# Silus of a Strassen-like first product queued behind the next copies, and one add ahead of the accumulators' sums

## The chip, the cores and the metric

The kernel runs on one core of a Trainium2 chip. The metric is the device time of one execution in microseconds (us). The numbers of the trace come from one profiled execution; its rows name TensorE as PE (its weight loads as PEld), VectorE as DVE, ScalarE as ACT, GpSimd as POOL, and the queue that issues DMAs as SP.

## The reference

Two blocks follow each other. The first is a chunked state-space scan over 4 batches of 8 heads with 768 positions; its output, laid out as 3072 tokens by 256 features, goes through a product to 2048 hidden features, the quick form of gelu, and a product back to 256.

```python
# per batch and head, chunk by chunk (32 positions), state is 16 x 32
L = np.exp(cum[:, :, :, None] - cum[:, :, None, :]) * causal
M = np.einsum('bhin,bhjn->bhij', Cc, Bc) * L
y = M @ xc + (Cc @ state) * exp(cum)
state = decay_full * state + sum_j(Bc_j xc_j * decay_from_j)
...
x = attn_out.transpose(0, 2, 1, 3).reshape(3072, 256)
h = x @ w_in                                  # 256 -> 2048
g = h * (1.0 / (1.0 + np.exp(-1.702 * h)))    # silu(1.702 h) / 1.702
out = (g @ w_out).astype(np.float32)          # 2048 -> 256
```

All is fp32.

## The kernel before

The 3072 tokens are worked off in six groups of 512 (g = 0 to 5). For each group the scan block makes yT (the tokens' features, transposed), the first product makes gT (the hidden features behind the silu), and the second product adds gT times w_out up in accumulators in PSUM. Within each engine the instructions run in the order in which the code is written; nothing reorders them. So the order is a matter of the strings of steps in the code.

Groups 2 to 5 do both products with seven instead of eight multiplications of half blocks (Winograd's form of Strassen's). The 2048 hidden features are eight pairs of blocks, j = 0 to 7. For one pair the first product has seven TensorE steps, written j.1, j.6, j.7, j.4 (into the PSUM tile X, one after the other; the partial sum after 1, 6 and 7 is copied by ScalarE to ac[0], b and ac[1], so that step 6 can't write X until the copy after step 1 has read it) and j.5, j.2, j.3 (into the PSUM tile Y). Step j.4 ends with a silu from X. Step j.D is no product: VectorE adds Y and ac into two quarters of gT, and ScalarE puts the silu over them. After j.3, which adds into Y once more and so must follow that add, VectorE adds Y and b into another quarter, and ScalarE puts the silu over it. Each TensorE step shows as two rows of 128x256 in the trace, since fp32 matmuls count double.

The second product of a pair is seven accumulations, each a P in the strings; they need gT and its differences, which VectorE makes in `mix_g` (tile mg, an M in the strings). Because P lags some pairs behind, the accumulations of the last two pairs of group g-1 stand among the first steps of group g. When they are all in, `combine` (C) adds the seven accumulators up: `copies` copies two of them on ScalarE (tile u), then VectorE does five adds (tiles u and c). `give` transposes c and stores it.

The PSUM holds one area of four banks that serves in turn as accumulators of a group (acc) and for the scan block's products cb (`score`; s1 and s2 in the strings); VectorE's `weigh` (w1, w2) multiplies cb into L. The other four banks rotate among X, Y and the rest (tag ff). y1 to y3 are the scan block's products that give yT of the next group. `decay` (2.3 us on VectorE) is called once per pass of the loop over the later pairs in groups 2 and 3. `clip_rows` and `decay_rows` make, once in group 2, the running product of a batch row of `a`, which `turn` needs for group 4 (tile since, read into CsT). The loads of later groups and the stores are issued by SP in the order of the code.

The start of a group, as it is before:

```python
run(g, "0.1 P P 0.6 P P 0.7 P 0.5 P 0.2 P 0.D", seven(g - 1, 6))
run(g, "1.1 P 0.4 P P 1.6 P P 0.3 M P P C 1.7 1.5 1.2 1.D", seven(g - 1, 7),
    M=lambda: mix_g(g, 0), C=lambda: combine(g - 1))
```

## Time and profile before

| what | value |
|---|---|
| median of 3 runs | 412.14 us (407.86 to 413.92) |
| the profiled execution | 409.75 us |
| its span, first to last instruction | 408.0 us |
| TensorE busy | 380.8 us, 93% of the span |
| VectorE busy | 272.5 us, 67% |
| ScalarE busy | 148.6 us, 36% |
| mean granted TensorE clock | 0.983 |

The profiled execution lies 2.4 us under the median. Rows of the timeline give the start from the span's beginning, the duration, engine, line, operation, tiles (out<-in), shape, how many instructions were merged, and in brackets the idle time before with the engine that ended it. In the clock line of the page a digit is the granted clock in tenths of full speed, in 40 slices of 10.2 us; 9 stands for full speed too.

### The profile page before, as it was taken

How to read it: one execution, taken by the hardware profiler on the slowest of the kernel's cores; microseconds unless marked ns; L12 is line 12 of the kernel's file. 1: busy time of each engine (PE TensorE's matmuls, PEld its weight loads, DVE VectorE, ACT ScalarE, POOL GpSimd, SP SyncE). 2: the span in 40 equal slices, each digit the busy share in tenths (PEclk: the TensorE clock that was granted, in tenths of full speed). 3: DMA queues.
4: the chain of work that ended last, by engine and by line, in shares of the span. 5: the costliest groups of instructions: out<-in, count | busy, mean ns of one | idle time of the engine just before them, and what ended most of it. 6: DMA issues, size and time to landing. Idle time of an engine off the chain costs nothing.

```text
span 408.0 us, 5632 instructions
## 1 busy us (share of the span) xinstructions
PE 380.8 (93%) x2216; PEld 282.3 (69%) x2216; DVE 272.5 (67%) x440; ACT 148.6 (36%) x330; POOL 10.4 (3%) x32
## 2 busy tenths in 40 slices
PE   6989999999999997899999699999699999689995
PEld 2444358885566786577878477888567888568885
DVE  3999999997799795446795456785454354433453
ACT  3338643303322222534333253433343432343430
POOL 5000000100000100000000000000000000000000
PEclk9999999999999999899999899999989999989999
DMA  8988947707683000085100062000010000000011
GB/s 140 234 233 196 287 154 85 222 12 132 139 169 116 16 24 0 26 185 101 51 2 2 0 119 90 0 0 2 0 53 0 2 1 0 2 0 0 2 51 51
DMA packets 85793, 29.55 MB, mean 72 GB/s; under 512 B 75720, under 2 KB 79240, under 8 KB 85768
## 3 DMA queue, kind: packets, MB, share of 16 engines
q1 hardware_dynamic: 85672, 29.07, 30.2%
q8 instruction: 17, 0.28, 0.3%
q10 hardware_dynamic: 96, 0.13, 0.1%
q14 instruction: 8, 0.07, 0.1%
HBM read 25.95 MB, written 3.24 MB: 72 GB/s over the span
## 4 chain that ended last, share of the span: by engine, by line
PE 80%; DVE 13%; issue 3%; ACT 2%; DMA 1%; POOL 0%; ACTq 0%; POOLq 0%; DVEq 0%
PE acc L742 27%; PE X L649 13%; PE h L593 13%; PE Y L659 10%; PE o L685 7%; PE cb L472 3%; DVE L L483 3%; PE y L549 2%; DVE gT L759 2%; PE y L540 1%; PE tp L436 1%; PE ab L331 1%; DVE c L759 1%; DVE u L759 1%; DVE mg L618 1%
## 5 line engine op out<-in xcount | busy, mean ns | idle before, releaser
L627 ACT ACTIVATE gT<-gT 128x512 f32<-128x512 f32 x64 | 33.5, 524 | 97.9 <-DVE gT L759 97.9
L742 PE MATMUL acc<-mg,mw 128*128 128x256 f32 x240 | 65.3, 379 | 0.0
L593 PE MATMUL h<-yT,w_in 128*128 128x512 f32 x128 | 57.4, 596 | 0.8 <-DVE w_in L186 0.8
L649 PE MATMUL X<-my,mi 128*128 128x256 f32 x128 | 41.9, 410 | 15.6 <-ACT ac L654 15.4
L759 DVE TENSOR_TENSOR gT<-Y,ac 128x512 f32<-128x512 f32 x32 | 22.0, 689 | 46.2 <-PE Y L659 45.4
L742 PEld LDWEIGHTS acc<-mg,mw 128*128 128x128 f32 x240 | 45.4, 190 | 6.1
L759 DVE TENSOR_TENSOR gT<-Y,b 128x256 f32<-128x256 f32 x32 | 13.5, 422 | 52.3 <-PE Y L659 52.3
L593 PEld LDWEIGHTS h<-yT,w_in 128*128 128x128 f32 x128 | 23.7, 190 | 29.3 <-issue 25.0
L742 PE MATMUL acc<-gT,w_out 128*128 128x256 f32 x160 | 43.8, 380 | 0.0
L323 DVE TENSOR_TENSOR_SCAN L<-a,idents 128x1024 f32<-128x1024 f32 x18 | 41.1, 2284 | 0.0
L649 PEld LDWEIGHTS X<-my,mi 128*128 128x128 f32 x128 | 23.1, 195 | 24.3 <-ACT ac L654 19.1
L654 ACT ACTIVATE ac<-X 128x256 f32<-128x256 f32 x64 | 24.1, 376 | 28.1 <-PE X L649 28.1
L596 ACT ACTIVATE gT<-h 128x512 f32<-128x512 f32 x32 | 19.0, 594 | 41.0 <-PE h L593 40.7
L742 PEld LDWEIGHTS acc<-gT,w_out 128*128 128x128 f32 x160 | 29.9, 190 | 5.3 <-issue 1.4
L483 DVE TENSOR_TENSOR L<-L,cb 128x2048 f32<-128x2048 f32 (+1 forms) x13 | 27.5, 2122 | 4.8 <-PE cb L472 4.3
L685 PE MATMUL o<-w_out,gT 128*128 128x256 f32 x128 | 29.3, 383 | 0.0
L618 DVE TENSOR_TENSOR mg<-gT 128x512 f32<-128x512 f32 x40 | 27.3, 683 | 1.9 <-ACT gT L627 1.9
L685 PEld LDWEIGHTS o<-w_out,gT 128*128 128x128 f32 x128 | 23.8, 190 | 4.1 <-issue 0.7
L742 PE MATMUL acc<-gT,mw 128*128 128x256 f32 x80 | 23.7, 382 | 0.0
L742 PE MATMUL acc<-mg,w_out 128*128 128x256 f32 x80 | 23.5, 379 | 0.0
L649 PE MATMUL X<-yT,w_in 128*128 128x256 f32 x64 | 19.7, 390 | 1.6 <-ACT yT L571 0.9
L659 PE MATMUL Y<-yT,mi 128*128 128x256 f32 x64 | 20.9, 411 | 0.0
(112 smaller groups left out, 518.7 us busy)
## 6 DMA issues: line engine op xcount, KB each, us to landing
a<-scratch SPq DMA_DIRECT2D x18, 512.0 KB, 5.8
bits<-in_moe_w_out_dram SPq DMA_DIRECT2D x4, 1024.0 KB, 7.1
x<-in_x_dram SPq DMA_DIRECT2D x24, 128.0 KB, 3.2
out_dram<-ob SPq DMA_DIRECT2D x11, 256.0 KB, 2.2
bits<-in_moe_w_in_dram SPq DMA_DIRECT2D x4, 512.0 KB
bits<-in_moe_w_in_dram SPq DMA_DIRECT2D x2, 1024.0 KB
b<-in_B_dram SPq DMA_DIRECT2D x24, 64.0 KB, 4.9
c<-in_C_dram SPq DMA_DIRECT2D x24, 64.0 KB, 2.8
```

The costliest lines, as they stand in the source:

```text
L323: nc.vector.tensor_tensor_scan(out=Ls[p][:, k].rearrange("p r q i -> p (r q i)"), data0=ra[n], data1=idents.rearrange("p h i -> p (h i)"), ...
L483: nc.vector.tensor_tensor(out=Lv[:, k], in0=Lv[:, k], in1=cb.rearrange("p r k e -> p k r e")[:, k], op=ALU.mult)
L593: nc.tensor.matmul(out=h, lhsT=w_in[:, k, f * P:(f + 1) * P], rhs=yT[g][:, k], start=(k == 0), stop=(k == NK - 1))
L596: nc.scalar.activation(gT[g, j][:, i], h, AF.Silu, scale=GELU_SCALE)
L618: nc.vector.tensor_tensor(out=t[:, 0:2], in0=B[:, :, 1], in1=B[:, 0], op=ALU.subtract)
L627: nc.scalar.activation(o, i, AF.Silu, scale=GELU_SCALE)
L649: nc.tensor.matmul(out=s["X"], lhsT=lhsT, rhs=rhs, start=i == "1", stop=i == "4", skip_group_check=True)
L654: nc.scalar.activation(copy, s["X"], AF.Copy)
L659: nc.tensor.matmul(out=o, lhsT=lhsT, rhs=rhs, start=s.pop("new", False), stop=i != "5", skip_group_check=True)
L685: nc.tensor.matmul(out=o[k // 2][:, k % 2], lhsT=gT[g, f // 2][:, f % 2, k * P:(k + 1) * P], rhs=w_out[:, f], start=(f == 0 and k % 2 == 0 ...
L742: nc.tensor.matmul(out=acc[g][0][i], lhsT=lhsT, rhs=rhs, start=(j == 0 and i in (0, 2, 5, 6)), stop=(j == NF // 2 - 1), skip_group_check=True)
L759: nc.vector.tensor_tensor(out=o, in0=v, in1=w, op=ALU.add)
```

## The change

The silu of j.D becomes a step of its own, j.S, and the silu after j.3 a step j.T. Both then stand later in the strings: S behind the next pair's step 1, T behind the next pair's step 7 (or a step near it). At a group's start 1.D is written ahead of C, 1.3 moves up behind 1.4, 0.3 moves up by one P, and 2.7 and 2.2 change places, as do 1.7 and a P. `clip_rows` and `decay_rows` move from behind pair 7 of group 2 to ahead of pair 4. Nothing is added or removed: each engine has as many instructions as before.

```diff
             if i == "3":
-                c12 = gT[g, j][:, 0, HT:]
-                plus(c12, s["Y"][:, 1], s["b"])
-                silu(c12, c12)
+                plus(gT[g, j][:, 0, HT:], s["Y"][:, 1], s["b"])
+        elif i == "T":
+            c12 = gT[g, j][:, 0, HT:]
+            silu(c12, c12)
         else:
-            block(g, j)
+            if i == "D":
+                block(g, j)
             c = gT[g, j].rearrange("p i (t e) -> p (i t) e", t=2)[:, 0:4:3]
-            plus(c, s["Y"], s["ac"])
-            silu(c, c)
+            if i == "D":
+                plus(c, s["Y"], s["ac"])
+            else:
+                silu(c, c)
...
-        run(g, "1.1 P 0.4 P P 1.6 P P 0.3 M P P C 1.7 1.5 1.2 1.D", seven(g - 1, 7),
+        run(g, "1.1 0.S P 0.4 P P 1.6 P 0.3 0.T M P P 1.7 P 1.5 1.2 1.D C", seven(g - 1, 7),
             M=lambda: mix_g(g, 0), C=lambda: combine(g - 1))
...
-            run(g, "2.1 1.4 2.6 2.5 2.7 2.2 1.3 s1 2.D w1 2.4 give 2.3 3.1 s2 w2 3.6 y1 3.7 y2 y3 3.5 "
-                "3.2 3.D", s1=lambda: score(n), w1=lambda: weigh(n), give=lambda: give(g - 1),
+            run(g, "2.1 1.S 1.4 1.3 2.6 2.5 2.2 2.7 1.T s1 2.D 2.S w1 2.4 give 2.3 3.1 2.T s2 w2 3.6 "
+                "y1 3.7 y2 y3 3.5 3.2 3.D", s1=lambda: score(n), w1=lambda: weigh(n), give=lambda: give(g - 1),
...
-            run(g, "P P 3.4 P P 3.3 P P P M", seven(g, 0), M=lambda: mix_g(g, 1))
+            run(g, "P P 3.S 3.4 P P 3.3 3.T P P P M", seven(g, 0), M=lambda: mix_g(g, 1))
+            for r in rows:
+                clip_rows(r)
+                decay_rows(r)
...
-            run(g, "2.1 1.4 2.6 2.5 2.7 2.2 1.3 2.D 3.1 2.4 3.5 3.6 2.3 3.2 3.7 3.D M",
+            run(g, "2.1 1.S 1.4 1.3 2.6 2.5 2.2 2.7 1.T 2.D 3.1 2.S 2.4 3.5 3.6 2.3 3.2 3.7 2.T 3.D M",
...
-            h = "{1}.1 P {0}.4 P {1}.6 P {0}.3 P {1}.7 P {1}.5 P {1}.2 P {1}.D M".format(j - 1, j)
+            h = "{1}.1 {0}.S P {0}.4 P {1}.6 P {0}.3 P {1}.7 {0}.T P {1}.5 P {1}.2 P {1}.D M".format(j - 1, j)
...
-        run(g, f"P P {k}.4 P P {k}.3 P P P", seven(g, 4))
+        run(g, f"P {k}.S P {k}.4 P P {k}.3 {k}.T P P P", seven(g, 4))
...
         mix_g(g, 6)
-        for b in rows:
-            clip_rows(b)
-            decay_rows(b)
```

What this does to ScalarE's queue at the start of group 3 (gT_0 and gT_1 are the group's first two pairs, ac and b the copies of X, u the copies of the accumulators), before:

```order
L627 ACTIVATE gT_0_1651<-gT_0_1651 128x256
L752 ACTIVATE u_1677<-acc_1373 128x2x256
L654 ACTIVATE ac_1_1655<-X_1_1654 128x256
L627 ACTIVATE gT_1_1690<-gT_1_1690 128x2x256
L654 ACTIVATE ac_2_1694<-X_2_1693 128x256
L627 ACTIVATE gT_1_1690<-X_1_1654 128x256
```

and with the change:

```order
L627 ACTIVATE gT_0_1651<-gT_0_1651 128x256
L655 ACTIVATE ac_1_1654<-X_1_1653 128x256
L757 ACTIVATE u_1684<-acc_1372 128x2x256
L655 ACTIVATE ac_2_1693<-X_2_1692 128x256
L627 ACTIVATE gT_1_1682<-gT_1_1682 128x2x256
L627 ACTIVATE gT_1_1682<-X_1_1653 128x256
```

The copy of 2.1 (ac_2) has changed places with silu 1.S (gT_1 over itself), and the copy of 1.7 (ac_1) with that of the accumulators.

VectorE's queue at the same place, from the last of mg_0 on, before:

```order
L620 TENSOR_TENSOR mg_0_1671<-gT_0_1651,mg_0_1671 128x256
L759 TENSOR_TENSOR u_1677<-acc_1373,u_1677 128x256
L759 TENSOR_TENSOR u_1677<-acc_1373,u_1677 128x512
L759 TENSOR_TENSOR c_1678<-u_1677 128x256
L759 TENSOR_TENSOR c_1678<-acc_1373,u_1677 128x512
L759 TENSOR_TENSOR c_1678<-acc_1373,u_1677 128x256
L759 TENSOR_TENSOR gT_1_1690<-Y_1_1687,ac_1_1655 128x2x256
```

and with the change:

```order
L620 TENSOR_TENSOR mg_0_1670<-gT_0_1651,mg_0_1670 128x256
L764 TENSOR_TENSOR gT_1_1682<-Y_1_1679,ac_1_1654 128x2x256
L764 TENSOR_TENSOR u_1684<-acc_1372,u_1684 128x256
L764 TENSOR_TENSOR u_1684<-acc_1372,u_1684 128x512
L764 TENSOR_TENSOR c_1685<-u_1684 128x256
L764 TENSOR_TENSOR c_1685<-acc_1372,u_1684 128x512
L764 TENSOR_TENSOR c_1685<-acc_1372,u_1684 128x256
```

The add of 1.D (gT_1) has moved from behind the five sums to ahead of them.

TensorE at the same place, from 1.4 to cb, before:

```order
L649 MATMUL X_1_1654<-my_1573,w_in 128x256
L649 MATMUL X_2_1693<-my_1573,mi_769 128x256
L659 MATMUL Y_2_1702<-my_1573,mi_769 128x256
L649 MATMUL X_2_1693<-my_1573,mi_769 128x256
L659 MATMUL Y_2_1702<-yT_1331,w_in 128x256
L659 MATMUL Y_1_1687<-yT_1331,mi_764 128x256
L472 MATMUL cb_1710<-CT_1568,BT_1566 128x256 x8
```

and with the change:

```order
L650 MATMUL X_1_1653<-my_1573,w_in 128x256
L660 MATMUL Y_1_1679<-yT_1331,mi_764 128x256
L650 MATMUL X_2_1692<-my_1573,mi_769 128x256
L660 MATMUL Y_2_1704<-my_1573,mi_769 128x256
L660 MATMUL Y_2_1704<-yT_1331,w_in 128x256
L650 MATMUL X_2_1692<-my_1573,mi_769 128x256
L472 MATMUL cb_1710<-CT_1568,BT_1566 128x256 x8
```

Step 1.3 (into Y_1) now stands directly behind 1.4, ahead of 2.6, and the last two steps into X_2 and Y_2 have changed places.

## The prediction

> **What bounds the kernel now.** I read the page first, then TensorE's waits, then the timeline of one start of a token group, then windows of the clock.

> ```profile
> span 408.0 us, 5632 instructions
> PE 380.8 (93%) x2216; PEld 282.3 (69%) x2216; DVE 272.5 (67%) x440; ACT 148.6 (36%) x330; POOL 10.4 (3%) x32
> PEclk9999999999999999899999899999989999989999
> PE 80%; DVE 13%; issue 3%; ACT 2%; DMA 1%; POOL 0%; ACTq 0%; POOLq 0%; DVEq 0%
> PE X L649 <- ACT ac L654: 15.4, 6, 3.6
> ```

> TensorE is busy for 93% of the span and holds 80% of the chain, so the time falls only where TensorE waits or runs slowly. The last row is from its waits (total, times, longest): of all its waiting behind other engines 15.4 us stand in six waits of an X product for a copy by ScalarE. The clock line has four 8s, in slices 17, 23, 30 and 36, one to each of groups 2 to 5. The timeline shows one of the long waits, at the start of group 3 (start, duration, engine and line, in brackets the idle time before):

> ```profile
> 222.45 0.59 PE L659 MATMUL Y<-yT,mi 128*128 128x256 f32 x2
> 223.08 0.42 DVE L759 TENSOR_TENSOR gT<-Y,b 128x256 f32<-128x256 f32 x1 [3.56 <-PE Y L659]
> 223.54 0.42 ACT L627 ACTIVATE gT<-gT 128x256 f32<-128x256 f32 x1 [1.37 <-DVE gT L759]
> 223.99 0.69 DVE L618 TENSOR_TENSOR mg<-gT 128x512 f32<-128x512 f32 x1 [0.48 <-ACT gT L627]
> 224.61 0.59 PE L659 MATMUL Y<-yT,w_in 128*128 128x256 f32 x2
> 225.04 0.59 PE L649 MATMUL X<-yT,w_in 128*128 128x256 f32 x2
> 225.47 0.59 PE L649 MATMUL X<-my,w_in 128*128 128x256 f32 x2
> 225.52 1.14 DVE L759 TENSOR_TENSOR u<-acc,u 128x256 f32<-128x256 f32 x2
> 227.97 0.68 DVE L759 TENSOR_TENSOR gT<-Y,ac 128x512 f32<-128x512 f32 x1
> 228.69 0.63 ACT L627 ACTIVATE gT<-gT 128x512 f32<-128x512 f32 x1 [3.87 <-DVE gT L759]
> 229.22 0.37 ACT L654 ACTIVATE ac<-X 128x256 f32<-128x256 f32 x1
> 229.64 0.70 PE L649 MATMUL X<-my,mi 128*128 128x256 f32 x2 [3.57 <-ACT ac L654]
> 233.67 1.22 PE L472 MATMUL cb<-CT,BT 32*128 32x256 f32 x16
> 234.97 2.29 DVE L483 TENSOR_TENSOR L<-L,cb 128x2048 f32<-128x2048 f32 x1 [0.17 <-PE cb L472]
> ```

> From the bottom up: product 2.6 (229.64) waits for the copy of 2.1 (229.22). That copy's input was ready long before: in these rows an engine that reads a product starts 0.63 us after the product does (222.45 to 223.08), so 225.04 + 0.63 = 225.67. But in ScalarE's queue silu 1.S stands ahead of it, and 1.S waits for add 1.D (227.97), which stands on VectorE behind the five sums of the accumulators (from 225.52). Step to step TensorE takes 0.43 us (225.04 to 225.47), so 2.6 was due at 225.90: it is 3.74 us late. Afterwards TensorE runs at half rate:

> ```profile
> 226.00:229.60 3.60, 0.07 (x1) 0.00 (x0) 2.62 (x5) 0.92 (x3) 0.00 (x0) 1.00 0.00 0
> 230.50:233.90 3.40, 3.40 (x12) 2.08 (x14) 0.12 (x1) 0.64 (x2) 0.00 (x0) 0.50 0.00 0
> ```

> Here the first pair of numbers behind the window is its length and TensorE's busy time; the third from the right is the granted clock. An empty stretch of 3.6 us is followed by 3.4 us at 0.50, which does 1.7 us less work.

> **The change at the start of a group.** I lay the new order over the same rows, with group 3's times.
> - TensorE, one step each 0.43 us: 0.3 comes one step earlier, at 222.02; 1.7 at 223.31; the last accumulation of the group before at 223.75; 1.5, 1.2, 2.1, 1.4 keep 224.18, 224.61, 225.04, 225.47; 1.3 is due at 225.90.
> - VectorE: the add of 0.3 begins at 222.02 + 0.63 = 222.65, silu 0.T 0.46 later (223.08 to 223.54) at 223.11, the three differences mg_0 0.45 after that, at 223.56; they take 225.52 - 223.99 = 1.53, to 225.09. Add 1.D follows a Y step by 0.71, so 224.61 + 0.71 = 225.32, for 0.61 to 0.69. The sums start at 225.93 and take 227.97 - 225.52 = 2.45: their last ends at about 228.45. So they are 0.4 us later than now.
> - ScalarE: copy 2.1 at 225.67, with no silu ahead of it that is still waiting. Product 2.6 follows a copy's start by 0.42 (229.22 to 229.64): 226.09 at the earliest. In its queue stands 1.3, which adds into the Y that 1.D reads, so it starts at 226.05 instead of 225.90, and 2.6 at 226.5, 2.5, 2.2, 2.7 at 226.9, 227.3, 227.8. Silus 1.S (0.72 after 1.D: 226.05) and 1.4 end before 2.6's copy is ready at 227.1, so 2.7 isn't held.
> - The next thing that is late is the cb products, due at 228.2: their PSUM area is that of the accumulators, and the sums must have read it. They start at about **228.5**, a new wait of 0.3.

> From there on nothing changes in relation to cb: the weighing (234.97, 1.30 after cb) has 1.3's and 2.D's adds ahead of it, which fit into 228.4 to 229.6; output copies, stores and the loads queued on SP behind the stores come as much sooner as the rest. So a group start gains 233.67 - 228.5 = **5.2 us**: 3.74 of the wait, and 1.88 between 2.6 and cb, where five steps now take 4.03 us instead of 2.15, less 0.45 for the two new short waits (0.15 at 1.3, 0.3 at cb). Groups 2, 3 and 4 have the same pattern: **15.5**. What I don't see is the price of cb behind the sums: none if the sums keep up, and up to 1.5 more if mg_0's 1.53 came between; I take 0.3, from 2.45 us of sums in these rows. For three groups that is -0.9 to +3.6 us.

> **The last group** has no cb products, and two more short waits:

> ```profile
> 356.15 0.70 PE L649 MATMUL X<-my,mi 128*128 128x256 f32 x2 [3.57 <-ACT ac L654]
> 362.30 0.70 PE L649 MATMUL X<-my,mi 128*128 128x256 f32 x2 [0.74 <-ACT ac L654]
> 364.00:366.00 2.00, 2.00 (x10) 1.44 (x8) 1.25 (x2) 1.24 (x3) 0.00 (x0) 1.00 0.00 0
> 366.43 0.70 PE L649 MATMUL X<-my,mi 128*128 128x256 f32 x2 [0.41 <-ACT ac L654]
> ```

> (The third row is a window's.) The times are group 3's plus 126.5 (356.15 against 229.64), so its 2.6 comes at 353.0. From there to 4.6 stand 15 steps (2.5, 2.2, 2.7, 3.1, 2.4, 3.5, 3.6, 2.3, 3.2, 3.7, 4.1, three between, 4.6) at 0.43, 6.45 us; one step, 2.4, waits 0.2 for the copy of 2.7. That makes 359.65 against 366.43: **6.8 us**, of which 5.5 are the pattern above without the wait at cb, and 1.15 the two short waits.

> **The scan of a's row** runs once, in group 2 (VectorE's rows; the X product is 0.1 of group 3):

> ```profile
> 181.56 0.42 DVE L620 TENSOR_TENSOR mg<-gT,mg 128x256 f32<-128x256 f32 x1
> 185.18 0.69 DVE L759 TENSOR_TENSOR gT<-Y,ac 128x512 f32<-128x512 f32 x1 [3.20 <-PE Y L659]
> 210.51 0.55 DVE L378 TENSOR_SCALAR af<-af 128x768 f32<-128x768 f32 x1
> 211.59 1.76 DVE L390 TENSOR_TENSOR_SCAN since<-af,first 128x768 f32<-128x768 f32 x1 [0.52 <-POOL af L383]
> 213.72 0.70 PE L649 MATMUL X<-yT,w_in 128*128 128x256 f32 x2 [0.79 <-DVE CsT L457]
> ```

> Clip, GpSimd's two small steps and scan take 213.35 - 210.51 = 2.84, and go into VectorE's idle 3.20 ahead of 4.D. That cover suffices by 0.36; were it gone, 4.D and its silu would come late by as much, with copy 5.1 now ahead of that silu. What goes is the wait of 0.79: **0.7**.

> **In the loop over the later pairs** the steps stay as they are on TensorE, which shows no wait there. I cost the moved silus at nothing; the cover is worked out under the slower rival. Step 1.D now takes its gT buffer ahead of u and c, so that 5.D reuses the buffer of gT_1 instead of u's. The last product that reads gT_1 is the third P of that pass, seven steps or 3.0 us ahead of 5.2, so this costs nothing either; without that cover it would be a fraction of those 3.0 us, once a group.

> **Sum.** 15.5 + 6.8 + 0.7 = 23.0 us. The profiled execution took 409.75, so its like would take 386.7. It lies 2.4 below the median of the runs, 412.14, which the same subtraction brings to 389.1. I take the middle, **388**.

> **Rivals.**
> - *The clock still drops.* Many short waits instead of one long one could keep a window poor enough for the half rate. Four windows at 1.7 stay: 388 + 6.8 = 395. Against it, 362.30 and 366.43 end waits of 0.74 and 0.41, and the window between them has clock 1.00. [...] The window at 1.00 speaks against it here. Chance 0.12.
> - *A new wait eats half.* If the sums are held until mg_0 and both adds are late, cb waits about as long as half of 2.6's wait now, with half of the clock's loss: 388 + 11 = 399. Chance 0.05.
> - *The change doesn't do what it says:* copy 2.1 waits for something else than 1.S, say its buffer, and 2.6 stays where it is: 410 to 412. Against it, the copy starts 0.53 after 1.S (228.69 to 229.22). Chance 0.05.
> - *Slower.* In the loop silu T now stands ahead of copy 1 of the pair after, and T waits for an add that VectorE runs behind a scan:

> ```profile
> 258.96 2.28 DVE L323 TENSOR_TENSOR_SCAN L<-a,idents 128x1024 f32<-128x1024 f32 x1
> 261.94 0.42 ACT L627 ACTIVATE gT<-gT 128x256 f32<-128x256 f32 x1 [2.20 <-DVE gT L759]
> 263.04 0.59 PE L649 MATMUL X<-yT,w_in 128*128 128x256 f32 x2
> ```

> T ends at 262.36; copy 1 is due at 263.04 + 0.63 = 263.67, so 1.3 us are spare. From that much lateness on, TensorE waits at step 6. Eight scans stand there (four in each of groups 2 and 3). If each came through whole, 2.28 and a half-rate window of 1.7, it would cost 32 us: 388 + 32 = 420. Nothing in the change makes VectorE later there, except the 2.84 of group 2, once. Chance 0.03.

> **Chances and range.** The forecast has 0.75 (384 to 392: 0.9 and 3.6 of the unknown, and 2.4 between profile and median). With the clock's rival the range is **384 to 396**, which leaves about 0.15 out. Two per cent of 412 is 8.2 us, about what a measurement of this kernel tells from no change: faster is 0.75 + 0.12 + 0.05 = 0.92, within 0.05, slower 0.03.

> **What would show it.** The rows of 2.6 have no wait over 0.5 us; the clock line has no 8 behind slice 10; ScalarE's copy of 2.1 stands ahead of 1.S; a short wait at cb, released by VectorE, stands in groups 2 to 4; 0.1 of group 3 doesn't wait for CsT. I am wrong if cb waits over 1.5 us, or if copies 1 in the loop come behind a late T.

## The result and the profile after

| | before | changed |
|---|---|---|
| median | 411.48 us of 4 runs (407.86 to 413.92; one run more than in the table before) | 386.77 us of 4 runs (386.59 to 388.83) |
| profiled execution | 409.75 us | 386.76 us |
| mean granted TensorE clock in it | 0.983 | 1.000 |

The ratio changed to before is 0.942, 95% interval 0.934 to 0.950: 22.99 us less by the two profiled executions. The same kernel timed again beside another one gave 386.86 us (386.7 to 388.76), ratio 0.943 (0.940 to 0.946).

From the page of the changed kernel the span, the busy times, the clock line and the chain; then the longest rows of TensorE's waits (total, times, longest):

```profile
span 385.1 us, 5634 instructions
PE 374.2 (97%) x2216; PEld 279.2 (72%) x2216; DVE 273.0 (71%) x440; ACT 147.2 (38%) x330; POOL 10.2 (3%) x32
PEclk9999999999999999999999999999999999999999
PE 93%; DVE 4%; issue 1%; ACT 1%; POOL 0%
```

```profile
PE tp L436 <- issue: 1.3, 1, 1.3
PE busy L349 <- DVE ones L250: 1.2, 1, 1.2
PE X L650 <- ACT yT L571: 0.9, 3, 0.3
```

TensorE's share of the chain rose from 80 to 93%, VectorE's fell from 13 to 4%. The page counts two instructions more than before, none of them on the five engines of its second row. The row of 15.4 us in which X waited for ScalarE's copy ac is gone, and what now leads the list are single waits of at most 1.3 us elsewhere. The four 8s of the clock line are gone too. TensorE's busy time fell by 6.6 us with the same 2216 matmuls: four windows of about 3.4 us at half rate, at the 1.7 each that the prediction worked out from the rows of before, would make 6.8.

The start of group 3 in the changed kernel, in the form in which the prediction shows it for before:

```profile
217.31 0.42 ACT L627 ACTIVATE gT<-gT 128x256 f32<-128x256 f32 x1 [0.94 <-DVE gT L764]
217.76 0.69 DVE L618 TENSOR_TENSOR mg<-gT 128x512 f32<-128x512 f32 x1 [0.48 <-ACT gT L627]
219.25 0.59 PE L650 MATMUL X<-yT,w_in 128*128 128x256 f32 x2
219.52 0.69 DVE L764 TENSOR_TENSOR gT<-Y,ac 128x512 f32<-128x512 f32 x1
220.12 1.14 DVE L764 TENSOR_TENSOR u<-acc,u 128x256 f32<-128x256 f32 x2
220.21 0.39 ACT L655 ACTIVATE ac<-X 128x256 f32<-128x256 f32 x1 [1.03 <-PE X L650]
220.26 0.70 PE L660 MATMUL Y<-yT,mi 128*128 128x256 f32 x2
220.49 0.62 ACT L627 ACTIVATE gT<-gT 128x512 f32<-128x512 f32 x1
220.80 0.59 PE L650 MATMUL X<-my,mi 128*128 128x256 f32 x2
221.64 1.01 DVE L764 TENSOR_TENSOR c<-acc,u 128x512 f32<-128x512 f32 x2
222.80 1.15 PE L472 MATMUL cb<-CT,BT 32*128 32x256 f32 x16
224.00 2.29 DVE L483 TENSOR_TENSOR L<-L,cb 128x2048 f32<-128x2048 f32 x1 [0.17 <-PE cb L472]
```

Read it along three steps. Copy 2.1 (220.21) has no silu ahead of it; what ended its idle time is the product itself. Product 2.6 (220.80) carries no wait: it comes 1.55 behind 2.1 (219.25), where before it came 4.60 behind (229.64 - 225.04). And cb comes 3.55 behind 2.1 instead of 8.63.

### The profile page after: what moved, and what is told of

The parts are those of the page before. It is cut to its first block, busy times and chain, and to the rows that moved or that the text cites. A ratio compares the mean times of both kernels' runs of the same rounds, so it can differ in the third digit from the quotient of the medians.

```text
span 385.1 us, 5634 instructions
## 1 busy us (share of the span) xinstructions
PE 374.2 (97%) x2216; PEld 279.2 (72%) x2216; DVE 273.0 (71%) x440; ACT 147.2 (38%) x330; POOL 10.2 (3%) x32
## 4 chain that ended last, share of the span: by engine, by line
PE 93%; DVE 4%; issue 1%; ACT 1%; POOL 0%
PE acc L747 32%; PE X L650 16%; PE h L593 14%; PE Y L660 11%; PE o L690 7%; PE cb L472 3%; PE y L549 3%; PE busy L349 1%; PE y L540 1%; PE tp L436 1%; DVE L L483 1%; PE oT L781 1%; PE ab L331 1%; DVE L L358 1%; PE A L500 1%
## 5 line engine op out<-in xcount | busy, mean ns | idle before, releaser
L627 ACT ACTIVATE gT<-gT 128x512 f32<-128x512 f32 x64 | 33.3, 520 | 30.5 <-DVE gT L764 30.5
L323 DVE TENSOR_TENSOR_SCAN L<-a,idents 128x1024 f32<-128x1024 f32 x18 | 41.1, 2282 | 0.0
L650 PE MATMUL X<-my,mi 128*128 128x256 f32 x128 | 39.3, 389 | 0.1
L483 DVE TENSOR_TENSOR L<-L,cb 128x2048 f32<-128x2048 f32 (+1 forms) x13 | 27.5, 2121 | 4.1 <-PE cb L472 3.7
L618 DVE TENSOR_TENSOR mg<-gT 128x512 f32<-128x512 f32 x40 | 27.3, 683 | 1.9 <-ACT gT L627 1.9
L571 ACT ACTIVATE yT<-y 128x256 f32<-128x256 f32 x24 | 7.9, 381 | 32.3 <-PE y L549 29.0
```

Source lines behind the costliest of these rows:

```text
L323: nc.vector.tensor_tensor_scan(out=Ls[p][:, k].rearrange("p r q i -> p (r q i)"), data0=ra[n], data1=idents.rearrange("p h i -> p (h i)"), ...
L483: nc.vector.tensor_tensor(out=Lv[:, k], in0=Lv[:, k], in1=cb.rearrange("p r k e -> p k r e")[:, k], op=ALU.mult)
L618: nc.vector.tensor_tensor(out=t[:, 0:2], in0=B[:, :, 1], in1=B[:, 0], op=ALU.subtract)
L627: nc.scalar.activation(o, i, AF.Silu, scale=GELU_SCALE)
L650: nc.tensor.matmul(out=s["X"], lhsT=lhsT, rhs=rhs, start=i == "1", stop=i == "4", skip_group_check=True)
```

## The experiments

**The add alone.** Before with one edit: `combine` behind 1.D. All silus, products and the scan stay as before.

```diff
-        run(g, "1.1 P 0.4 P P 1.6 P P 0.3 M P P C 1.7 1.5 1.2 1.D", seven(g - 1, 7),
+        run(g, "1.1 P 0.4 P P 1.6 P P 0.3 M P P 1.7 1.5 1.2 1.D C", seven(g - 1, 7),
```

> The kernel before with one edit: at a group's start C stands behind 1.D, so the add of 1.D goes ahead of the five sums; every silu, product and the scan stay where they were. My theory (the wait goes as soon as VectorE has the add first, but silu 1.S still stands ahead of the copies of the accumulators and of 2.1 on ScalarE): by the rows of before the add begins at 225.5, 1.S at 226.2, the copies u at 226.8, copy 2.1 at 227.3, product 2.6 at 227.7, 1.8 us late instead of 3.7, cb at 230.0 instead of 233.7. That is 3.6 us a start, 14.6 for four: 395 us, if 1.8 us of waiting leave the clock at full rate; 402 if each start still has its half-rate window. The rival that the add alone is the whole change gives 387; the rival that the silus are gives 410.

Measured: 397.0 us (395.87 to 398.14, 4 runs), ratio 0.964 (0.957 to 0.970); profiled 396.09. Of its wait rows and page, then of its timeline at group 3 (its 2.1 starts at 221.76):

```profile
PE X L649 <- ACT ac L654: 7.6, 6, 1.6
PEclk9999999999999999999999999999999999999999
```

```profile
222.96 0.63 ACT L627 ACTIVATE gT<-gT 128x512 f32<-128x512 f32 x1 [1.48 <-DVE gT L759]
223.50 0.58 ACT L752 ACTIVATE u<-acc 128x512 f32<-128x512 f32 x1
223.97 0.38 ACT L654 ACTIVATE ac<-X 128x256 f32<-128x256 f32 x1
224.40 0.70 PE L649 MATMUL X<-my,mi 128*128 128x256 f32 x2 [1.61 <-ACT ac L654]
```

Copy 2.1 still stands behind silu 1.S, and now behind the copies u as well, so 2.6 still waits, 1.61 instead of 3.57. But the waits halve (15.4 to 7.6) and with waits of 1.6 every half-rate window at a group's start is gone: 13.7 us for one moved step (409.75 - 396.09), of which 7.8 are waiting; the other 5.9 are close to the 6.8 of four windows. The expectation, 395 us with the clock at full rate, came about. So the moved add brings more than half of the whole gain by itself.

**The silus alone.** The changed kernel with `combine` back ahead of 1.D, and the order of the products at a group's start and the place of the scan as before.

```diff
-        run(g, "1.1 0.S P 0.4 P P 1.6 P 0.3 0.T M P P 1.7 P 1.5 1.2 1.D C", seven(g - 1, 7),
+        run(g, "1.1 0.S P 0.4 P P 1.6 P P 0.3 0.T M P P C 1.7 1.5 1.2 1.D", seven(g - 1, 7),
...
-            run(g, "2.1 1.S 1.4 1.3 2.6 2.5 2.2 2.7 1.T s1 2.D 2.S w1 2.4 give 2.3 3.1 2.T s2 w2 3.6 "
+            run(g, "2.1 1.S 1.4 2.6 2.5 2.7 2.2 1.3 1.T s1 2.D 2.S w1 2.4 give 2.3 3.1 2.T s2 w2 3.6 "
...
```

> The change without its moves on VectorE and TensorE: the silus are steps S and T at their new places, but at a group's start C stays ahead of 1.D, 1.3, 0.3, 1.7, 2.7 and 2.2 keep their old places, and the scan keeps its own. My theory: copy 2.1 gets ahead of 1.S and 2.6 starts in time, but the copy of 2.6 stands behind 1.S, which still waits for the add behind the sums; so the wait moves to 2.7 (at 230.0 by the rows of before, 3.1 us of waiting instead of 3.6), and the half-rate window stays. Gain about 1 us a start: 405 us. The rival that the silus' places are what counts gives 390 or less.

Measured: 403.83 us (402.09 to 404.7, 4 runs), ratio 0.979 (0.974 to 0.985). Waits and clock line, then group 3's start:

```profile
PE X L650 <- ACT b L655: 10.2, 4, 2.6
PEclk9699999999999999899999999999999999989999
```

```profile
229.97 0.63 ACT L627 ACTIVATE gT<-gT 128x512 f32<-128x512 f32 x1 [2.29 <-DVE gT L764]
230.77 0.38 ACT L655 ACTIVATE b<-X 128x256 f32<-128x256 f32 x1
231.20 0.70 PE L650 MATMUL X<-my,mi 128*128 128x256 f32 x2 [2.33 <-ACT b L655]
```

The wait has moved from 2.6 to 2.7: the copy b of 2.6 now stands behind silu 1.S, which still waits for the late add. In groups 2, 4 and 5 product 2.6 waits for nothing and 2.7 waits 2.61; in group 3, shown here, 2.6 still waits 0.38 and 2.7 waits 2.33. The silus' place decides which copy is caught, the add's place how long it is caught. Two of the four starts, those of groups 2 and 5, are still followed by a half-rate window (the 8s; the 6 in slice 2 belongs to the last section); a window behind every start had been expected.

**The order of the products.** The changed kernel with the steps behind 2.1 in their old order.

```diff
-            run(g, "2.1 1.S 1.4 1.3 2.6 2.5 2.2 2.7 1.T s1 2.D ...
+            run(g, "2.1 1.S 1.4 2.6 2.5 2.7 2.2 1.3 1.T s1 2.D ...
```

> The changed kernel with TensorE's steps behind 1.4 in their old order (2.6, 2.5, 2.7, 2.2, 1.3 instead of 1.3, 2.6, 2.5, 2.2, 2.7) at the four group starts; queues of the silus, the sums and the scan stay changed. My theory: copy b of 2.6 stands behind 1.S and 1.4's silu and starts some 0.6 us late, so 2.7 waits 0.8 us; the new waits of 0.1 at 1.3 and 0.3 at cb go, so a start with cb loses 0.3 and the last one 0.7: 388.4 us. The rival that this order is only a matter of taste gives 386.8; the rival that 1.3's add, now behind the weighing's inputs, makes cb's weighing late gives 390 or more.

Measured: 388.17 us (387.78 to 390.07, 4 runs) against 386.86 for the changed kernel timed beside it: 1.3 us. In group 3 product 2.6 waits 0.38 for copy 2.1, and cb starts 4.07 behind 2.1 (223.58 - 219.51) instead of 3.55, which is 0.52 more. In groups 2 and 4 it starts 3.79 behind 2.1 (164.17 - 160.38 and 282.72 - 278.93), 0.24 more, and in the last group 4.6 comes 8.66 behind 2.1 (344.94 - 336.28) instead of 8.34, 0.32 more: together 1.3. The amount came near the expected 1.6, but not from the wait of 0.8 at 2.7 that was expected: 2.7 starts 0.64 behind 2.5 at each start, 0.2 more than a step.

**The scan back in its place.**

```diff
-            for r in rows:
-                clip_rows(r)
-                decay_rows(r)
...
         mix_g(g, 6)
+        for b in rows:
+            clip_rows(b)
+            decay_rows(b)
```

> The changed kernel with clip_rows and decay_rows put back behind pair 7 of group 2. My theory: step 0.1 of group 3 waits 0.8 us for CsT again, 0.7 us more than the changed kernel: 387.5 us, all in that one place. The rival that the scan in the middle of group 2 delayed 4.D and cost what it saved gives 386.8 or less.

Measured: 389.55 us (387.42 to 389.58, 4 runs). Three of these ran at a mean clock of 0.990, the profiled one, 387.42, at 0.998. Its waits of TensorE have the row that before has and the changed kernel hasn't:

```profile
PE X L650 <- DVE CsT L457: 0.8, 1, 0.8
```

Profiled execution against profiled execution it is 0.7 us longer (387.42 against 386.76). The median's other 2.1 us go with the lower mean clock of the three other runs, which were not profiled; the last section has profiles in which a like amount stands far from the scan.

**The loop's silus back.** In the loop over the later pairs, and for the pairs that lead into and out of it, silu S goes again right behind its add, and T behind its add.

```diff
-            h = "{1}.1 {0}.S P {0}.4 P {1}.6 P {0}.3 P {1}.7 {0}.T P {1}.5 P {1}.2 P {1}.D M".format(j - 1, j)
+            h = "{1}.1 P {0}.4 P {1}.6 P {0}.3 {0}.T P {1}.7 P {1}.5 P {1}.2 P {1}.D {1}.S M".format(j - 1, j)
...
-            run(g, "4.1 y1 4.6 4.5 y2 4.7 4.2 y3 4.D M", y1=b[0], y2=b[1], y3=b[2],
+            run(g, "4.1 y1 4.6 4.5 y2 4.7 4.2 y3 4.D 4.S M", y1=b[0], y2=b[1], y3=b[2],
...
-            run(g, "2.1 1.S 1.4 1.3 2.6 2.5 2.2 2.7 1.T 2.D 3.1 2.S 2.4 3.5 3.6 2.3 3.2 3.7 2.T 3.D M",
+            run(g, "2.1 1.S 1.4 1.3 2.6 2.5 2.2 2.7 1.T 2.D 3.1 2.S 2.4 3.5 3.6 2.3 3.2 3.7 2.T 3.D 3.S M",
...
-        run(g, f"P {k}.S P {k}.4 P P {k}.3 {k}.T P P P", seven(g, 4))
+        run(g, f"P P {k}.4 P P {k}.3 {k}.T P P P", seven(g, 4))
```

> The changed kernel with the silus of the loop over the later pairs (S of pairs 3 to 7 in the last group, 4 to 7 in the others, and T in the loop) put back directly behind their adds; the start of a group stays changed. My theory: the loop is bound by TensorE, so this costs nothing: 386.8 us within 0.5, except at the last group's start, where copy 4.1 gets behind 3.S again and 4.6 may wait some 0.4 us. The rival that the loop's silus carry part of the gain gives 390 or more.

Measured: 388.59 us (387.2 to 391.41, 4 runs; the two at clock 0.999 and 1.000 gave 387.2 and 387.58). Its waits have one row for a copy ac again, at the last group's 4.6:

```profile
PE X L650 <- ACT ac L655: 0.4, 1, 0.4
```

So of all the silus moved outside a group's start, those around this single step are worth something: 0.4 us of waiting, and 0.56 on the way from 2.1 to 4.6 (344.25 - 335.35 = 8.90, against 8.34). In the loops of groups 2 to 5 TensorE's wait rows show no wait for a copy of X or a silu in either order. The two runs at full clock are 0.4 and 0.8 us above the changed kernel's 386.8, so at most some tenths are left that no row places.

**The add held back step by step.** The changed kernel with n idle adds on VectorE ahead of 1.D, at each of the four starts; they add two pieces of w_in into a tile that nothing reads, so the output stays the same.

```diff
+    def hold(n):
+        for _ in range(n):
+            nc.vector.tensor_tensor(out=spare, in0=w_in[:, 0, :P], in1=w_in[:, 1, :P], op=ALU.add)
...
-        run(g, "... 1.7 P 1.5 1.2 1.D C", seven(g - 1, 7),
+        run(g, "... 1.7 P 1.5 1.2 E 1.D C", seven(g - 1, 7), E=lambda: hold(5),
```

With 5, 10 and 15 of them:

> The changed kernel with five idle adds of 128x128 (of w_in into a spare tile that nothing reads) on VectorE ahead of 1.D, at each of the four group starts. At some 0.24 us each they make 1.D, and with it TensorE's step 1.3, about 1.0 us late. My theory, in which a start costs what TensorE waits and a short wait leaves the clock alone: four times 1.0 us, 390.8 us, clock 1.00 throughout. The rival that short waits already bring the half rate: 390.8 + up to 6.8.

> As the one with five, with ten idle adds: step 1.3 is about 2.2 us late, four times: 395.6 us by the waits alone. The runs so far had no half-rate window at a wait of 1.6 us, two in four starts at 2.7 us in two pieces, four in four at 3.6 us; so I expect none to two of them here, 395.6 to 399.

> As the one with five, with fifteen idle adds: step 1.3 is about 3.4 us late, four times: 400.4 us by the waits alone. My theory expects the half-rate window behind at least three of the four waits, 1.7 us each: 405.5 to 407.2. The rival that the half rate in the kernel before came from something else at the group's start (the accumulators' area, the output copies) gives 400.4 with clock 1.00.

Measured: medians of 393.69 us (two runs, 391.5 and 395.89), 404.75 (two runs, 403.16 and 406.35), and 413.86 (412.07 to 416.49, 8 runs); the ratios to before are 0.960 (0.952 to 0.968), 0.987 (0.979 to 0.995) and 1.009 (1.005 to 1.014). The sizes were missed because an idle add takes more than the 0.24 I had reckoned with, and with ten of them because three drops of the clock came instead of none to two. Five of them in the timeline with 5, and TensorE's wait at 1.3 in the three kernels in turn (there are no other long ones):

```profile
224.60 1.59 DVE L973 TENSOR_TENSOR spare<-w_in 128x128 f32<-128x128 f32 x5
```

```profile
PE Y L660 <- DVE gT L764: 5.1, 4, 1.3
```

```profile
PE Y L660 <- DVE gT L764: 11.6, 4, 2.9
```

```profile
PE Y L660 <- DVE gT L764: 18.1, 4, 4.5
```

An add takes 0.32 (1.59 / 5). The clock lines of the kernels with 10 and with 15:

```profile
PEclk9599999999999999899999999999989999989999
```

```profile
PEclk9999999999999999799999899999989999979999
```

With 10 three of the four starts are followed by a drop, with 15 all four, two of them for two windows (the 7s); the 5 in slice 2 belongs to the last section. The line of the kernel with 5 has such a 5 there too, and no drop at any start. With the waits as measured, the prediction's prices (a wait in full, 1.7 for each window) give 386.8 + 5.1 = 391.9, 386.8 + 11.6 + 3 × 1.7 = 403.5 and 386.8 + 18.1 + 6 × 1.7 = 415.1. The first two lie within 0.4 of the lower runs, 391.5 and 403.16, but those were not profiled, so the count of windows in them isn't known; the third is 2.7 over its profiled execution, 412.35. Each profiled execution can be priced by itself, with the waits above and with TensorE's busy time from its page (378.7, 381.9 and 382.1 us, where the changed kernel has 374.2): 386.8 + 5.1 + 4.5 = 396.4, 386.8 + 11.6 + 7.7 = 406.1 and 386.8 + 18.1 + 7.9 = 412.8, against 395.89, 406.35 and 412.35. So with 15 the six windows cost 7.9 and not 10.2: in the first window of each double drop TensorE was still waiting for a part of the time (busy 1.06 and 2.10 us of 3.41). Half of that busy time and 1.7 for each of the other four windows come to 8.4, so by my estimate the half rate adds to the busy time alone and nothing to a wait. The main thing stands: lateness of this one add, with nothing else touched, brings back both the wait and the clock's loss, up to the time of before.

**A version meant to be faster.** At a group's start 1.7, 1.5, 1.2 and the add go ahead of the last accumulation, and mg_0 goes later, behind the second weighing (in the last group behind 2.D).

```diff
-        run(g, "1.1 0.S P 0.4 P P 1.6 P 0.3 0.T M P P 1.7 P 1.5 1.2 1.D C", seven(g - 1, 7),
-            M=lambda: mix_g(g, 0), C=lambda: combine(g - 1))
+        run(g, "1.1 0.S P 0.4 P P 1.6 P 0.3 0.T P P 1.7 1.5 1.2 1.D P C", seven(g - 1, 7),
+            C=lambda: combine(g - 1))
...
-            run(g, "2.1 1.S 1.4 1.3 2.6 2.5 2.2 2.7 1.T s1 2.D 2.S w1 2.4 give 2.3 3.1 2.T s2 w2 3.6 "
+            run(g, "2.1 1.S 1.4 1.3 2.6 2.5 2.2 2.7 1.T s1 2.D 2.S w1 2.4 give 2.3 3.1 2.T s2 w2 M 3.6 "
...
-            run(g, "2.1 1.S 1.4 1.3 2.6 2.5 2.2 2.7 1.T 2.D 3.1 ...
+            run(g, "2.1 1.S 1.4 1.3 2.6 2.5 2.2 2.7 1.T 2.D N 3.1 ...
```

> A version that may beat the changed kernel: at a group's start 1.7, 1.5 and 1.2 go ahead of the last accumulation, and the differences mg_0 go from ahead of 1.D to behind the second weighing (in the last group behind 2.D). The add of 1.D then begins some 0.4 us sooner, step 1.3 no longer waits for it (0.1 us), and the sums end 0.4 us sooner, so that cb no longer waits for them (0.3 us). Theory: 0.4 us a start, 385.3 us. The rival that the copies u on ScalarE, now behind a later accumulation, hold the sums instead gives 386.8 or more.

Measured: 386.41 us (385.81 to 388.62, 6 runs), ratio 0.943 (0.938 to 0.947). By the medians it is not to be told from the changed kernel; at like clocks it is a little faster: its four runs at 0.999 and 1.000 took 385.81 to 386.61 (mean 386.2), the six of the changed kernel at 1.000 took 386.59 to 386.92 (mean 386.8). Now copies u wait for the last accumulation and the sums for the copies:

```profile
221.64 0.60 ACT L757 ACTIVATE u<-acc 128x512 f32<-128x512 f32 x1 [0.91 <-PE acc L747]
222.27 1.15 DVE L764 TENSOR_TENSOR u<-acc,u 128x256 f32<-128x256 f32 x2 [0.30 <-ACT u L757]
PE cb L472 <- DVE c L764: 0.7, 2, 0.4
```

The rival's mechanism shows at the starts with cb: what VectorE saves comes too late for the sums, and cb still waits up to 0.4 for them. From 1.2 to cb these three starts take 4.38 to 4.44 us, the accumulation that now stands between included; in the changed kernel it is 3.98, and 4.41 with such a step of 0.43. So they gained nothing. The last group's start has no cb: from 1.2 to 4.6 it takes 8.95 (345.43 - 336.48) instead of 8.77 + 0.43 = 9.20, 0.25 less. Where the rest of the 0.6 lies isn't settled, and neither the 385.3 of the theory nor the 386.8 of the rival is the time.

## Why the prediction was right

The sum was 409.75 - 23.0 = 386.7 for an execution like the profiled one; it took 386.76. By its steps, with the rows of 2.1 and cb in groups 2 and 4, of before and of changed:

```profile
160.07 0.59 PE L649 MATMUL X<-yT,w_in 128*128 128x256 f32 x2
168.70 1.27 PE L472 MATMUL cb<-CT,BT 32*128 32x256 f32 x16
289.09 0.59 PE L649 MATMUL X<-yT,w_in 128*128 128x256 f32 x2
297.32 1.81 PE L472 MATMUL cb<-CT,BT 32*128 32x256 f32 x16
```

```profile
160.36 0.59 PE L650 MATMUL X<-yT,w_in 128*128 128x256 f32 x2
163.91 1.15 PE L472 MATMUL cb<-CT,BT 32*128 32x256 f32 x16
278.13 0.59 PE L650 MATMUL X<-yT,w_in 128*128 128x256 f32 x2
281.68 1.15 PE L472 MATMUL cb<-CT,BT 32*128 32x256 f32 x16
```

1. *The starts, 15.5 predicted.* From 2.1 to cb it takes 3.55 in each of the three groups, instead of 8.63, 8.63 and 8.23, and cb itself takes 0.12, 0.07 and 0.66 less, because the half-rate window of before, which ended at 169.0, 233.9 and 298.7, reached into it. That is 5.20, 5.15 and 5.34, together 15.69.
2. *The new short waits, 0.15 at 1.3 and 0.3 at cb.* Due at 219.25 + 2 × 0.43 = 220.11, 1.3 starts at 220.26: 0.15. Four steps behind 2.6 cb was due at 220.80 + 4 × 0.43 = 222.52 and starts at 222.80: 0.28, just behind the last sum (221.64 + 1.01 = 222.65). All three starts fell to the value taken, not to the ends of its range.
3. *The copy in ScalarE's queue is the cause.* Taking either half of the change back shows it: with the add early and the copy behind the silu 2.6 waits 1.61, with the copy ahead and the add late (and the products in their old order, which costs only 1.3 us by itself) 2.7 waits 2.33 to 2.61. With everything else changed, idle adds that make the add late bring the wait back in step with their number (up to 1.3, 2.9 and 4.5 us with 5, 10 and 15).
4. *The last group, 6.8 predicted.* Its 2.1 in before, then its 2.1 and its 4.6 in the changed kernel:

```profile
351.55 0.59 PE L649 MATMUL X<-yT,w_in 128*128 128x256 f32 x2
```

```profile
335.23 0.59 PE L650 MATMUL X<-yT,w_in 128*128 128x256 f32 x2
343.57 0.59 PE L650 MATMUL X<-my,mi 128*128 128x256 f32 x2
```

   From 2.1 to 4.6 it takes 8.34 instead of 14.88 (366.43 - 351.55): 6.54. Of the 0.26 short of 6.8, 0.1 is 2.6, which comes 1.55 behind 2.1 where I had worked out 1.45. These 0.26 too much and the 0.19 too little at the starts nearly cancel in the sum.
5. *The scan, 0.7 predicted.* The gain at 2.1 of the last group is 351.55 - 335.23 = 16.32. The first start's 2.1 came 0.29 later than in before (160.36 against 160.07), so 16.32 + 0.29 - 15.69 = 0.92 were gained between the starts: the wait of 0.79 for CsT, and 0.13 that no row places. The experiment gave 0.7 back. The cover was as thin as said:

```profile
178.04 1.76 DVE L390 TENSOR_TENSOR_SCAN since<-af,first 128x768 f32<-128x768 f32 x1 [0.52 <-POOL af L383]
180.25 0.69 DVE L764 TENSOR_TENSOR gT<-Y,ac 128x512 f32<-128x512 f32 x1 [0.45 <-PE Y L660]
```

   Add 4.D (180.25) still finds 0.45 us of idle time behind the scan, against 0.36 worked out.
6. *The loop's silus, nothing predicted.* Right for the loop; the 0.4 at the last group's 4.6 were counted among its two short waits.
7. *The rivals.* The clock keeps 1.00 across starts with waits of 0.15 and 0.28, and even with 1.6 (the add alone). Several short waits at one start brought no half rate: no start of the changed kernel is followed by a drop. The slower rival did not come up either: no copy 1 in the loop stands behind a late T.
8. *The step that was not needed* is the last: I went from 386.7 halfway to 389.1 because the profiled execution of before lay 2.4 under its median. Three of four runs of the changed kernel lie at 386.6 to 386.8, at clock 1.000. The runs' spread goes with the mean clock (the last section), so an execution is to be set against one at a like clock elsewhere, not against the median. The forecast of 388 was 1.2 over for it.

## What to carry to other kernels

In an engine that runs its queue in the order of the code, as ScalarE does in these traces, ask of each instruction ahead of a copy that frees PSUM what it waits for: here a silu that waited for a VectorE add held the copy, and through it TensorE for 3.57 us, because that add stood behind 2.45 us of sums. Cure both ends, since here the order of ScalarE alone only moved the wait to the next copy, and the order of VectorE alone only shortened it. Count TensorE's waits with what the clock takes behind them: here it nearly added half to the price of a wait of 3.6 us, nothing to one of 1.6, and in between, at 2.6 to 2.9, it came or stayed away by where the wait lay (the next section).

## What the hardware showed beyond that

So here it is the place on this grid that tells like waits apart. Below are windows of the kernel with 10 idle adds, cut along its grid, first around group 2's wait of 2.89, then two for the same wait in group 3; behind the length stands TensorE's busy time:

```profile
164.46:167.88 3.42, 0.56 (x3) 0.16 (x1) 3.15 (x11) 0.38 (x1) 0.00 (x0) 1.00 0.00 0
225.90:229.32 3.42, 2.38 (x12) 1.75 (x10) 3.15 (x10) 1.36 (x3) 0.00 (x0) 1.00 0.01 2
229.32:232.73 3.41, 1.55 (x7) 1.40 (x8) 3.24 (x9) 1.28 (x3) 0.00 (x0) 1.00 0.00 0
```

In group 2 one window holds the whole wait, and the next runs at half rate. In group 3 two windows share it, and no drop follows. Over the four starts of before and of the kernels with the silus alone and with 5, 10 and 15 idle adds, the window at full rate just ahead of a drop has TensorE busy for 0.20 to 1.57 us of 3.41, and every window around a wait without a drop has 1.55 or more. That a limit lies near there is my estimate from these windows. (The kernel with the add alone has no drop, so its grid isn't known.)

**Half rate near the start of some executions.** Both kernels vary from run to run with the mean clock: the changed one 386.6 to 386.8 at 1.000 and 388.83 at 0.991, before 408.0 at 0.987, 409.8 at 0.983 and 412.2 at 0.974. In four profiled executions, those with the silus alone, with 5 and with 10 idle adds and with mg_0 later, there was a stretch at half rate that begins at 10.5 to 11.7 us and lasts two or three windows, while the DMA engines are 94 to 96% busy; they are so in the changed kernel too, without a drop (in before, the count of windows at the starts may vary as well; its other runs were not profiled). The window of 10 to 20 us in the changed kernel, and in the one with mg_0 later:

```profile
10.00:20.00 10.00, 9.17 (x61) 4.65 (x65) 9.69 (x15) 4.01 (x10) 0.78 (x2) 1.00 0.96 240
```

```profile
10.00:20.00 10.00, 10.00 (x48) 4.76 (x49) 9.43 (x13) 2.38 (x5) 0.78 (x2) 0.66 0.95 237
```

At 0.66 TensorE did 48 matmuls there instead of 61. An execution with this stretch, compared with one at a clock near 1, shows time that no edit made: with mg_0 later 388.62 against 386.2, with 5 idle adds, where the stretch lasts three windows, 395.89 against 391.5. So the price of the scan's place could be read only from executions at nearly the same clock. With 10 idle adds and with the silus alone the stretch begins on the grid of the later drops, 46 windows ahead of the first of them. But TensorE's busy time in the window ahead doesn't tell here: 1.59, 1.62, 2.27 and 2.34 us with the stretch, 1.80 to 1.97 in the changed kernel, before and the kernel with 15 idle adds without it. What sets it off in one run and not in the next stays open.
